# Third layer's opening: layer-norm statistics in two tiles, twelve token tiles normalised ahead of the last output products, first chunk in the blocks' order

## The chip, the core and the metric

The kernel runs on one core of one Trainium2 chip. A core has five engines that run their own queues in order: PE (matrix products; its weight loads are listed apart as PEld), DVE (vector work), ACT (activation functions and scaled copies), POOL and SP (here both mostly issue transfers). All data that the engines work on lie in an on-chip memory of 128 partitions; PE writes to a second, small one (PSUM), from which DVE and ACT read. The metric is the device time of one execution in microseconds, as the median of several runs.

## What is computed

Four layers on one sequence of L = 2048 tokens with D = 640 channels, each with a residual: a long convolution (a state-space model, evaluated with Fourier transforms), attention with 32 query heads of 20 channels that share one key and one value head, the same convolution again, the same attention again.

```python
    x = A_u
    x = x + _A_ref(_layernorm(x, axis=-1), A_A_re, A_A_im, A_B_re, A_B_im, A_C_re, A_C_im, A_log_dt, A_Dskip)
    x = x + _B_ref(_layernorm(x, axis=-1), B_wq, B_wk, B_wv, B_wo)
    x = x + _A_ref(_layernorm(x, axis=-1), A_A_re, A_A_im, A_B_re, A_B_im, A_C_re, A_C_im, A_log_dt, A_Dskip)
    x = x + _B_ref(_layernorm(x, axis=-1), B_wq, B_wk, B_wv, B_wo)
    return x
```

The layer norm has no weights: (x − mean) / sqrt(var + eps), with mean and variance over a token's 640 channels.

## The kernel before

**Where things lie.** x stays on the chip for the whole program, as 16 token tiles `x[:, t]` of 128 tokens by 640 channels. Each layer opens pools of tiles and gives them back at its end. Within a pool the places follow the order in which the code first asks for each tag, and a tile that is asked for waits only for the former tiles that lay in its own place. The layers' pools start at the same address. In the second layer (attention, `nm` = "b") there lie, in bytes per partition from that address: keys, values and queries up to 27,712; then the output weights `wo` (12,800) and `wol` (2,560); six probability tiles `pt` (24,576 together); two `on` tiles (4,096); two `rc` tiles (4,096); ten `ot` tiles (20,480). In the third layer (convolution, "c") the order before is B 16,384; R 8,192; xn 12,288; A1 16,384; kh 16,384; wi 32,768; A2 and A0 16,384 each. So xn lies on queries and `wo`, kh on `pt` and the first `on`, and wi on the second `on`, `rc` and `ot`.

**The end of an attention layer** (`main_loop`, L1128). The queries go in four blocks `nb` of four token tiles each; block `nb` owns the tiles `TAUS[4*nb : 4*nb+4]`, and with `FIRST = (0, 2, 1, 3)` these are the tiles t with t % 4 equal to `FIRST[nb]`. Per step PE computes scores (L1173), ACT exponentials (L1177) and PE the weighted values (L1187). Output products of the block before run one at a time between the steps, and `add` (L1230) adds each into x on DVE (L1235) and, when a tile is complete, calls `stats` (L625), which writes mean and variance of the tile into `mv` (L630, L631). Thus all tiles with t % 4 of 0, 2 and 1 are complete early in the last block, and only the four with t % 4 == 3 are left for the end. There, after the last exponential, `normalize_last` (L1219) divides the last heads on DVE (`rcl`, `onl`); PE meanwhile runs the other 28 output products (weights `wo`), then 16 with `onl` (weights `wol`), both at L1247 into the tiles `pl`; and eight additions with their statistics follow as the pairs of products end. The tiles `pl` 0 to 2 share the tag "s2" of three PSUM buffers with the tiles z of the convolution.

**The opening of a convolution layer** (`conv_layer`, L737). `norm` (L694) works on all 16 tiles at once: it adds eps (L705), takes the root on ACT (L687), a reciprocal with one correction step on DVE (L688 to L692), the offset (L707), and the negated scale and offset (L750, L751). Then for each chunk c of 128 channels `prepare` (L820) normalises the 16 token tiles into `xn` on ACT (L761; one buffer), `raw` (L563) runs four groups t of 32 products by the Fourier weights `wf` on PE (L574) into a PSUM tile z, and ACT copies each z into the spectrum A (L576). Group t reads the tiles t, t + 4, t + 8 and t + 12, so the group t = 3 reads the four last tiles. Chunks 0 and 1 use `raw`, later ones `dense`. `whole` gives DVE the work behind it: `halve` (L580) in four pieces for chunk 0, piece i after copy i, then the transform `fft8` (L114, L117), then the multiplication by the kernel's spectrum (L845 and on), whose tile kh is loaded on SP's queue at L711. The inverse transform's weights `wi` follow in the same queue (L555).

**What sets the order.** In `conv_layer` PE, ACT and DVE run in the order of the code. In `main_loop` PE and ACT do; DVE's order is worked out by a planner, which takes instructions in the code's order as they become ready in its own model of time. SP's queue is in order.

Of the kernel before, what the change touches and what calls it, by code (L numbers as in the profile page):

```python
# [11 lines left out]
F32 = mybir.dt.float32  # L12
# [3 lines left out]
AF = mybir.ActivationFunctionType  # L16
# [141 lines left out]
class Net:  # L158
# [7 lines left out]
    def setup(self, ctx):  # L166
# [8 lines left out]
        self.mv = self.xp.tile([P, 16, 2], F32, name="mv")  # L175
# [382 lines left out]
    def spectrum(self, nm, k):  # L558
        tag = f"A{k}" if k < 3 else "kh"
        return self.cvp.tile([P, 16, 256], F32, tag=tag, bufs=1, name=f"A{nm}")  # L560

    def raw(self, xn, nm, k):
# [4 lines left out]
        for t in range(4):  # L567
# [12 lines left out]
    def halve(self, A, pieces=1):  # L580
# [3 lines left out]
        for i in range(pieces):  # L584
# [5 lines left out]
    def whole(self, A, sg, pieces=1):  # L590

        return self.halve(A, pieces) + fft8(self.nc, A, self.B, sg, low=self.B[:, 8:16])
# [32 lines left out]
    def stats(self, t):  # L625
# [5 lines left out]
        nc.vector.bn_aggr(self.mv[:, t], st.rearrange("p a b -> p (a b)"))  # L631
# [62 lines left out]
    def norm(self, nm):  # L694
        rs = self.xp.tile([P, 16], F32, tag="rs", bufs=2, name=f"rs{nm}")
        nmr = self.xp.tile([P, 16], F32, tag="nmr", bufs=2, name=f"nmr{nm}")
        self.rstd(self.xp, self.mv, rs, nmr, 16)
        return rs, nmr

    def rstd(self, pool, mv, out, nmr, n):  # L700

        nc = self.nc
        ve = pool.tile([P, n], F32, tag="ve", bufs=2, name="ve")
        sq = pool.tile([P, n], F32, tag="sq", bufs=2, name="sq")
        nc.vector.tensor_scalar(ve, mv[:, :, 1], EPS, None, ALU.add)  # L705
        self.root(ve, sq, out)
        nc.vector.scalar_tensor_tensor(nmr, mv[:, :, 0], -1.0, out, op0=ALU.mult, op1=ALU.mult)  # L707
# [30 lines left out]
    def conv_layer(self, nm, first):  # L738
# [6 lines left out]
        with tc.manual_schedule(engines={mybir.EngineType.PE, mybir.EngineType.Activation,  # L745
                                         mybir.EngineType.DVE}):
            rs, nmr = self.norm(nm)
            rsm = self.xp.tile([P, 16], F32, tag="rsm", bufs=1, name=f"rsm{nm}")
            nmrm = self.xp.tile([P, 16], F32, tag="nmrm", bufs=1, name=f"nmrm{nm}")
            nc.vector.tensor_scalar(rsm, rs, -1.0, None, ALU.mult)  # L750
            nc.vector.tensor_scalar(nmrm, nmr, -1.0, None, ALU.mult)  # L751
            self.norm_next(nm)
            if first:
                self.kernel_spectra()
            R = self.scratch(nm)
# [4 lines left out]
            def normal(out, c, tau, r, b):  # L760
                nc.scalar.activation(out, X(c, tau), AF.Identity, scale=r[:, tau : tau + 1],  # L761
# [617 lines left out]
```

## Time and profile before

| | |
|---|---|
| median of 3 runs | 3023.3 us |
| lowest and highest | 3022.26 and 3024.99 us |
| profiled execution, its own time | 3024.13 us |
| its span in the profile | 3022.3 us |
| PE busy | 2769.4 us (92%) |
| ACT busy | 2421.5 us (80%) |
| DVE busy | 1384.6 us (46%) |
| mean granted PE clock | 0.951 |
| third layer, from the last product of the second to the fourth layer's first transposition | 1695.3 to about 1936.5 us |

All numbers but the first two rows are from one profiled execution. Times within it count from the start of its span. In its timeline a row gives the start, the duration, the engine, the line of the code, the operation with what it writes and reads, the count, and in brackets how long the engine had been idle before and what ended that wait. The granted clock is the share of PE's full clock that the chip allowed in a stretch. Matrix products are pipelined, so a busy PE is not PE at its peak.

### The profile page before, as it was taken

The numbers are of one execution on the slowest core, as the hardware profiler recorded it, in microseconds if no ns is written. First come the engines' busy times: TensorE is split into PE (matmuls) and PEld (weight loads), VectorE is DVE, ScalarE is ACT, GpSimd is POOL, SyncE is SP. The second block draws the span as 40 slices with busy tenths as digits, with TensorE's granted clock in tenths as the row PEclk, the third lists the DMA queues.
The fourth block names the chain that finished last, engine by engine and source line by source line (L and its number), as shares of the span: only waits on it lengthen the run. The fifth ranks groups of instructions, "written<-read, shape, count | busy, mean of one in ns | idle before, by whom it ended". The sixth has DMA issues, their size and how long they took to land. (4 is left out here: it accounts for less than half of the span.)

```text
span 3022.3 us, 52462 instructions
## 1 busy us (share of the span) xinstructions
PE 2769.4 (92%) x21696; PEld 1266.8 (42%) x21696; DVE 1384.6 (46%) x1784; ACT 2421.5 (80%) x2894; POOL 86.3 (3%) x149
## 2 busy tenths in 40 slices
PE   2676978898999999999999888798999999999999
PEld 0333978775233323333233678673233233333233
DVE  7999899942122232322323499721222223222223
ACT  5888351444999999999999524238999999999997
POOL 0001001000000000000000011000000000000000
PEclk9656999999999999999999989899999999999999
DMA  6114555433200010100000256131100100110100
GB/s 145 33 22 112 175 154 112 97 116 115 81 22 25 22 27 21 27 24 23 25 22 20 86 112 145 39 130 56 28 24 23 43 22 25 39 28 21 43 19 23
DMA packets 126000, 175.60 MB, mean 58 GB/s; under 512 B 59460, under 2 KB 81988, under 8 KB 122132
## 3 DMA queue, kind: packets, MB, share of 16 engines
q1 hardware_dynamic: 102680, 137.70, 15.7%
q0 software_dynamic: 21104, 33.45, 5.5%
q8 instruction: 175, 2.87, 0.4%
q10 hardware_dynamic: 1968, 0.98, 0.1%
q14 instruction: 73, 0.60, 0.1%
HBM read 95.22 MB, written 48.04 MB: 47 GB/s over the span
## 5 line engine op out<-in xcount | busy, mean ns | idle before, releaser
L1177 ACT ACTIVATE pt<-scd 128x1024 f32<-128x1024 f32 x1024 | 942.2, 1116 | 6.9 <-PE scd L1173 5.5
L1177 ACT ACTIVATE pt<-scb 128x1024 f32<-128x1024 f32 x1024 | 942.1, 1116 | 6.5 <-PE scb L1173 5.1
L1187 PE MATMUL pod<-pt,vt 128*32 128x512 f32 x4096 | 546.9, 606 | 4.4 <-DVE on L1204 0.2
L1187 PE MATMUL pob<-pt,vt 128*32 128x512 f32 x4096 | 546.4, 605 | 4.4
L1173 PE MATMUL scb<-qpb,kt 62*128 62x512 f32 x2048 | 385.8, 451 | 5.9 <-DVEq L1122 5.6
L1173 PE MATMUL scd<-qpd,kt 62*128 62x512 f32 x2048 | 385.7, 451 | 5.9 <-PEq L1122 5.5
L1173 PEld LDWEIGHTS scd<-qpd,kt 62*128 62x128 f32 x2048 | 166.1, 185 | 402.2 <-ACT pt L1177 392.4
L1173 PEld LDWEIGHTS scb<-qpb,kt 62*128 62x128 f32 x2048 | 166.1, 185 | 401.6 <-ACT pt L1177 391.9
L1235 DVE TENSOR_TENSOR x<-pyd,x 128x320 f32<-128x320 f32 x146 | 71.8, 492 | 560.7 <-PE pyd L1247 560.7
L1235 DVE TENSOR_TENSOR x<-pyb,x 128x320 f32<-128x320 f32 x146 | 71.8, 492 | 547.5 <-PE pyb L1247 547.5
L1207 DVE RECIPROCAL rc<-rc 128x512 f32<-128x512 f32 x62 | 207.9, 3353 | 2.1
L1187 PEld LDWEIGHTS pod<-pt,vt 128*32 128x32 f32 x4096 | 80.6, 108 | 177.4 <-issue 159.5
L1187 PEld LDWEIGHTS pob<-pt,vt 128*32 128x32 f32 x4096 | 80.6, 108 | 177.5 <-issue 159.5
L804 PE MATMUL yc<-Ac,wi 128*128 128x128 f32 x640 | 80.2, 291 | 32.1 <-DVE Ac L114 20.4
L804 PE MATMUL ya<-Aa,wi 128*128 128x128 f32 x640 | 79.8, 290 | 32.2 <-DVE Aa L114 22.8
L1247 PE MATMUL pyb<-wo,ot 128*32 128x320 f32 x1168 | 105.3, 432 | 0.0
L1247 PE MATMUL pyd<-wo,ot 128*32 128x320 f32 x1168 | 105.3, 432 | 0.0
L804 PEld LDWEIGHTS yc<-Ac,wi 128*128 128x128 f32 x640 | 79.7, 207 | 34.9 <-DVE x L815 11.8
L804 PEld LDWEIGHTS ya<-Aa,wi 128*128 128x128 f32 x640 | 79.1, 206 | 35.1 <-DVE Aa L114 24.0
L610 ACT ACTIVATE Aa<-za 128x1024 f32<-128x1024 f32 x12 | 12.3, 1025 | 101.6 <-PE za L608 101.6
L608 PE MATMUL zc<-xnc,wf 128*128 128x256 f32 x384 | 85.3, 384 | 2.4 <-ACT xnc L761 2.3
L608 PE MATMUL za<-xna,wf 128*128 128x256 f32 x384 | 83.7, 380 | 2.7 <-ACT xna L761 2.7
(323 smaller groups left out, 3110.3 us busy)
## 6 DMA issues: line engine op xcount, KB each, us to landing
Akh<-kh SPq DMA_DIRECT2D x10, 2048.0 KB
kh<-Ak SPq DMA_DIRECT2D x5, 2048.0 KB
qhd<-qh SPq DMA_DIRECT2D x40, 256.0 KB
qld<-ql SPq DMA_DIRECT2D x40, 256.0 KB
qpb<-qhd SPq DMA_DIRECT2D x256, 40.0 KB
qpd<-qhd SPq DMA_DIRECT2D x256, 40.0 KB
ot<-on SPq DMA_DIRECT2D x216, 40.0 KB
wf<-in_c_wf POOLq DMA_DIRECT2D x16, 512.0 KB, 8.0
```

What stands on the lines that cost most here:

```text
L608: nc.tensor.matmul(zv[:, :, c, kk], self.wf[:, t + 4 * h, j, c, kk], x, start=(n == 0), stop=(n == 3))
L610: nc.scalar.activation(A.rearrange("p (o s) d -> p o s d", o=2)[:, :, 2 * t : 2 * t + 2], z.rearrange("p (c o e) -> p o c e", c=2, o=2), A ...
L804: nc.tensor.matmul(y[:, s * DC : (s + 1) * DC], self.wi[:, t, j, c_, kk], v[:, 2 * t + c_, kk], start=(i == 0 and not whole), stop=(i == 3 ...
L1173: nc.tensor.matmul(sc[:, 512 * par : 512 * par + 512], kt[rows, 128 * t : 128 * t + 128], qps[nb, hg, pr][rows], start=True, stop=True)
L1177: nc.scalar.activation(pt, sc, AF.Exp, scale=SCALE)
L1187: nc.tensor.matmul(po[32 * j : 32 * j + 32], vt[:, t], pts[step, j // 2][:, 512 * (j % 2) : 512 * (j % 2) + 512], start=(t == 0), stop=(t ...
L1207: nc.vector.reciprocal(rc, rc)
L1235: nc.vector.tensor_tensor(xh, py, xh, ALU.add)
L1247: nc.tensor.matmul(py[j : j + m], o[:, 128 * i + j : 128 * i + j + m], w[:, 320 * half : 320 * half + 320], start=start, stop=stop)
```

## The change

`mv` becomes two tiles: `mv[0]` for the twelve token tiles with t % 4 in (0, 1, 2) and `mv[1]` for the four with t % 4 == 3; `place` maps a token tile to its tile and column. `norm(nm, g)` works on one of the two sets and also makes the negated scale and offset. In the first layer both sets are done where the one was. For the third layer `norm("c", 0)` stands at the end of the second layer's `main_loop`, after `normalize_last` and ahead of the last output products. In the third layer the tiles A1, A2 and xn are asked for ahead of R, kh and wi, so that the order of places becomes B, A1, A2, xn, R, kh, wi, A0. Chunk 0 is prepared in the order FIRST: the tiles of the groups 0 and 2 are normalised first, those of group 1 ahead of the first group's z, and, after that z and its copy, `norm("c", 1)` and the four tiles of group 3; `halve` takes its four pieces in the same order. Later chunks and the other layers keep their order.

```diff
--- before.py
+++ after.py
@@ -172,7 +172,9 @@
         nc.vector.memset(self.halfpi, 0.5 * math.pi)
         self.xp = ctx.enter_context(tc.tile_pool(name="xp", bufs=1))
         self.x = self.xp.tile([P, 16, D], F32, name="x")
-        self.mv = self.xp.tile([P, 16, 2], F32, name="mv")
+        self.mv = [self.xp.tile([P, 12, 2], F32, name="mv0"), self.xp.tile([P, 4, 2], F32, name="mv1")]
+        self.rn = None
+        self.placed = {}
         self.kd = self.dr.tile([NCH, P, 16 * DC], F32, name="kd")
         self.kh = self.dr.tile([NCH, P, 32 * DC], F32, name="kh")
 
@@ -556,15 +558,18 @@
                           self.ins[name][:, t * 1024 : (t + 1) * 1024])
 
     def spectrum(self, nm, k):
+        if nm in self.placed:
+            return self.placed.pop(nm)
         tag = f"A{k}" if k < 3 else "kh"
         return self.cvp.tile([P, 16, 256], F32, tag=tag, bufs=1, name=f"A{nm}")
 
-    def raw(self, xn, nm, k):
+    def raw(self, xn, nm, k, order=range(4), ahead=lambda t: None):
 
 
         nc = self.nc
         A = self.spectrum(nm, k)
-        for t in range(4):
+        for t in order:
+            ahead(t)
             z = self.ps2(f"z{nm}_{t}")
             zv = z.rearrange("p (h c k d) -> p h c k d", h=2, c=2, k=2)
             for h in (1, 0):
@@ -577,19 +582,19 @@
                                  z.rearrange("p (o c d) -> p o c d", o=2, c=2), AF.Copy)
         return A
 
-    def halve(self, A, pieces=1):
+    def halve(self, A, pieces=1, order=None):
 
 
         calls, n = [], 8 // pieces
-        for i in range(pieces):
+        for i in range(pieces) if order is None else order:
             lo, hi = A[:, n * i : n * i + n], A[:, 8 + n * i : 8 + n * i + n]
             for op, o in ((ALU.add, self.B[:, 8 + n * i : 8 + n * i + n]), (ALU.subtract, hi)):
                 calls.append(lambda o=o, lo=lo, hi=hi, op=op: self.nc.vector.tensor_tensor(o, lo, hi, op))
         return calls
 
-    def whole(self, A, sg, pieces=1):
-
-        return self.halve(A, pieces) + fft8(self.nc, A, self.B, sg, low=self.B[:, 8:16])
+    def whole(self, A, sg, pieces=1, order=None):
+
+        return self.halve(A, pieces, order) + fft8(self.nc, A, self.B, sg, low=self.B[:, 8:16])
 
     def dense(self, xn, nm, k):
 
@@ -628,7 +633,12 @@
         st = self.xp.tile([P, 2, 6], F32, tag="st", bufs=2, name=f"st{t}")
         for h in range(2):
             nc.vector.bn_stats(st[:, h], self.x[:, t, 320 * h : 320 * h + 320])
-        nc.vector.bn_aggr(self.mv[:, t], st.rearrange("p a b -> p (a b)"))
+        g, i = self.place(t)
+        nc.vector.bn_aggr(self.mv[g][:, i], st.rearrange("p a b -> p (a b)"))
+
+    def place(self, t):
+
+        return (1, t // 4) if t % 4 == 3 else (0, 3 * (t // 4) + t % 4)
 
     def stats_setup(self, nm):
 
@@ -691,20 +701,22 @@
         nc.vector.tensor_scalar(sq, sq, -0.5, 1.5, ALU.mult, ALU.add)
         nc.vector.tensor_tensor(out, out, sq, ALU.mult)
 
-    def norm(self, nm):
-        rs = self.xp.tile([P, 16], F32, tag="rs", bufs=2, name=f"rs{nm}")
-        nmr = self.xp.tile([P, 16], F32, tag="nmr", bufs=2, name=f"nmr{nm}")
-        self.rstd(self.xp, self.mv, rs, nmr, 16)
-        return rs, nmr
-
-    def rstd(self, pool, mv, out, nmr, n):
-
-        nc = self.nc
-        ve = pool.tile([P, n], F32, tag="ve", bufs=2, name="ve")
-        sq = pool.tile([P, n], F32, tag="sq", bufs=2, name="sq")
+    def norm(self, nm, g):
+
+        nc, n = self.nc, (12, 4)[g]
+        if g == 0:
+            self.rn = {}
+        rs, nmr, rsm, nmrm = (self.xp.tile([P, n], F32, tag=f"{k}{g}", bufs=1, name=f"{k}{g}{nm}")
+                              for k in ("rs", "nmr", "rsm", "nmrm"))
+        ve = self.xp.tile([P, n], F32, tag=f"ve{g}", bufs=1, name=f"ve{g}{nm}")
+        sq = self.xp.tile([P, n], F32, tag=f"sq{g}", bufs=1, name=f"sq{g}{nm}")
+        mv = self.mv[g]
         nc.vector.tensor_scalar(ve, mv[:, :, 1], EPS, None, ALU.add)
-        self.root(ve, sq, out)
-        nc.vector.scalar_tensor_tensor(nmr, mv[:, :, 0], -1.0, out, op0=ALU.mult, op1=ALU.mult)
+        self.root(ve, sq, rs)
+        nc.vector.scalar_tensor_tensor(nmr, mv[:, :, 0], -1.0, rs, op0=ALU.mult, op1=ALU.mult)
+        nc.vector.tensor_scalar(rsm, rs, -1.0, None, ALU.mult)
+        nc.vector.tensor_scalar(nmrm, nmr, -1.0, None, ALU.mult)
+        self.rn[g] = rs, nmr, rsm, nmrm
 
     def load_spectrum(self, c):
         A = self.spectrum(f"kh{c}", 3)
@@ -744,32 +756,37 @@
         tt = nc.vector.tensor_tensor
         with tc.manual_schedule(engines={mybir.EngineType.PE, mybir.EngineType.Activation,
                                          mybir.EngineType.DVE}):
-            rs, nmr = self.norm(nm)
-            rsm = self.xp.tile([P, 16], F32, tag="rsm", bufs=1, name=f"rsm{nm}")
-            nmrm = self.xp.tile([P, 16], F32, tag="nmrm", bufs=1, name=f"nmrm{nm}")
-            nc.vector.tensor_scalar(rsm, rs, -1.0, None, ALU.mult)
-            nc.vector.tensor_scalar(nmrm, nmr, -1.0, None, ALU.mult)
+            if first:
+                self.norm(nm, 0)
+                self.norm(nm, 1)
             self.norm_next(nm)
             if first:
                 self.kernel_spectra()
+            else:
+                for c in range(2):
+                    self.placed[f"{nm}{c}"] = self.spectrum(f"{nm}{c}", c + 1)
+                self.placed["xn"] = self.cvp.tile([P, 24, DC], F32, tag="xn", bufs=1, name=f"xn{nm}0")
             R = self.scratch(nm)
 
             def X(c, tau):
                 return self.x[:, tau, c * DC : (c + 1) * DC]
 
-            def normal(out, c, tau, r, b):
-                nc.scalar.activation(out, X(c, tau), AF.Identity, scale=r[:, tau : tau + 1],
-                                     bias=b[:, tau : tau + 1])
+            def normal(out, c, tau, neg=0):
+                g, i = self.place(tau)
+                r, b = self.rn[g][2 * neg : 2 * neg + 2]
+                nc.scalar.activation(out, X(c, tau), AF.Identity, scale=r[:, i : i + 1], bias=b[:, i : i + 1])
 
             def normals(xn, c, t):
 
                 for j in range(2):
                     i = 4 * j + t
-                    normal(xn[:, i], c, 8 * j + t, rs, nmr)
-                    normal(xn[:, 8 + 2 * i], c, 8 * j + t + 4, rs, nmr)
-                    normal(xn[:, 9 + 2 * i], c, 8 * j + t + 4, rsm, nmrm)
+                    normal(xn[:, i], c, 8 * j + t)
+                    normal(xn[:, 8 + 2 * i], c, 8 * j + t + 4)
+                    normal(xn[:, 9 + 2 * i], c, 8 * j + t + 4, 1)
 
             def new_xn(c):
+                if "xn" in self.placed:
+                    return self.placed.pop("xn")
                 return cv.tile([P, 24, DC], F32, tag="xn", bufs=1, name=f"xn{nm}{c}")
 
             def m(a, c_):
@@ -820,10 +837,26 @@
             def prepare(c):
 
                 xn = new_xn(c)
+
+                def group(t):
+                    for tau in (t + 4, t + 12, t, t + 8):
+                        normal(xn[:, tau], c, tau)
+
+                if c == 0 and not first:
+                    for t in FIRST[:2]:
+                        group(t)
+
+                    def ahead(t):
+                        if t == FIRST[0]:
+                            group(FIRST[2])
+                        elif t == FIRST[1]:
+                            self.norm(nm, 1)
+                            group(FIRST[3])
+
+                    return self.raw(xn, f"{nm}{c}", 1, FIRST, ahead)
                 for t in range(4):
                     if c < 2:
-                        for tau in (t + 4, t + 12, t, t + 8):
-                            normal(xn[:, tau], c, tau, rs, nmr)
+                        group(t)
                     else:
                         normals(xn, c, t)
                 return (self.raw if c < 2 else self.dense)(xn, f"{nm}{c}", (c + 1) % 3)
@@ -833,7 +866,7 @@
             self.wi = cv.tile([P, 8, 2, 2, 2, P], F32, tag="wi", name="wi")
             self.load_weights(self.wi, "c_wi", nc.sync)
             As[1] = prepare(1)
-            weave(self.whole(As[0], -1, 4), ())
+            weave(self.whole(As[0], -1, 4, None if first else FIRST), ())
 
             def spread(A, kh):
 
@@ -1275,6 +1308,8 @@
                 if (nb, hg, t) == (0, 1, 0):
                     late_loads(pts[steps[s + 2], 0])
             on = normalize_last()
+            if out is None:
+                self.norm("c", 0)
 
             last = []
             for g in range(3):
```

## The prediction

> **What bounds the kernel now.** I read the page first, then the chain of waits in order of time, then the timeline of the place where the second layer (attention) hands over to the third (convolution), then the windows of that place.
>
> ```profile
> span 3022.3 us, 52462 instructions
> ...
> PE 25%; issue 6%; DVE 1%; SPq 0%; DMA 0%; ACT 0%; POOL 0%; POOLq 0%; ACTq 0%
> ```
> ```profile
> 2057.69 1.95 ACT pt L1177 x2
> ```
>
> The first is the chain's share by engine, the second its earliest entry. The shares add to about a third of the span, which fits a chain that begins at 2057.69: it says nothing of the handover, which has to be read from the timeline (start, duration, engine, line, count, idle time before).
>
> ```profile
> 1682.15 1.28 ACT L687 ACT_TABLE_LOAD   x1
> ...
> 1683.18 7.80 PE L1247 MATMUL plb<-wo,ot 128*128 128x320 f32 x28
> ...
> 1683.32 0.73 DVE L1224 STREAM_SHUFFLE rcl<-pob 128x512 f32<-128x512 f32 x1
> 1683.35 0.36 SPq L711 DMA_DIRECT2D Akh<-kh  x1
> ...
> 1687.48 0.69 DVE L1227 TENSOR_TENSOR onl<-pob,rcl 128x512 f32<-128x512 f32 x1
> ...
> 1690.82 4.47 PE L1247 MATMUL plb<-wol,onl 128*128 128x320 f32 x16
> 1692.10 0.89 DVE L1235 TENSOR_TENSOR x<-plb,x 128x320 f32<-128x320 f32 x2 [3.93 <-PE plb L1247]
> ...
> 1695.32 3.98 SPq L555 DMA_DIRECT2D wi<-in_c_wi  x8
> ...
> 1697.51 0.44 DVE L1235 TENSOR_TENSOR x<-plb,x 128x320 f32<-128x320 f32 x1
> ...
> 1698.77 0.21 DVE L631 BATCH_NORM_AGGREGATE mv<-st 128x2 f32<-128x12 f32 x1
> 1699.01 0.17 DVE L705 TENSOR_SCALAR ve<-mv 128x16 f32<-128x16 f32 x1
> 1699.22 0.21 ACT L687 ACTIVATE sq<-ve 128x16 f32<-128x16 f32 x1 [15.79 <-DVE ve L705]
> ...
> 1700.80 0.17 DVE L751 TENSOR_SCALAR nmrmc<-nmrc 128x16 f32<-128x16 f32 x1
> 1700.85 6.26 ACT L761 ACTIVATE xnc<-x,nmrc,rsc 128x128 f32<-128x128 f32 x16 [1.42 <-DVE rsmc L750]
> ...
> 1701.40 16.87 PE L574 MATMUL zc<-xnc,wf 128*128 128x128 f32 x128 [6.11 <-ACT xnc L761]
> 1707.63 1.02 ACT L576 ACTIVATE Ac<-zc 128x1024 f32<-128x1024 f32 x1 [0.52 <-ACT xnc L761]
> ...
> 1711.16 1.02 ACT L576 ACTIVATE Ac<-zc 128x1024 f32<-128x1024 f32 x1 [2.50 <-PE zc L574]
> ...
> 1718.30 1.02 ACT L576 ACTIVATE Ac<-zc 128x1024 f32<-128x1024 f32 x1 [2.55 <-PE zc L574]
> 1719.22 6.26 ACT L761 ACTIVATE xnc<-x,nmrc,rsc 128x128 f32<-128x128 f32 x16
> ...
> 1719.76 14.72 PE L574 MATMUL zc<-xnc,wf 128*128 128x128 f32 x128 [1.49 <-ACT xnc L761]
> ...
> 1731.88 1.23 DVE L845 SCALAR_TENSOR_TENSOR Rc<-Ac,Akh 128x1024 f32<-128x1024 f32 x1
> ```
>
> The last output products end at 1690.82 + 4.47 = 1695.29. PE then waits 6.11 us for a strictly serial chain: last additions into x (to 1697.95), last statistics (to 1698.98), root and scales of all 16 token tiles, first normalised tiles. Nothing else runs under it: ACT had been idle for 15.79 us. From 1701.40 PE sets the pace: the four z groups of chunk 0 are copied out at 1707.63, 1711.16 and so on to 1718.30.
>
> Three of those steps take 3.55 us each (1718.30 − 1707.63 = 10.67), but the first group, from 1701.40 to 1707.6, took 6.2 us. The windows (stretch, its length, busy time and count of PE, weight load, DVE, ACT and POOL, granted clock, DMA share, GB/s) say why.
>
> ```profile
> 1699.00:1700.00 1.00, 0.00 (x0) 0.00 (x0) 0.64 (x4) 0.21 (x1) 0.00 (x0) 0.72 1.03 422
> ...
> 1706.00:1707.00 1.00, 1.00 (x10) 1.00 (x9) 0.00 (x0) 1.00 (x3) 0.00 (x0) 0.86 1.00 385
> ```
> ```profile
> 1774.00:1779.00 5.00, 0.00 (x0) 0.00 (x0) 4.90 (x6) 2.88 (x8) 1.66 (x2) 0.90 0.00 0
> ...
> 1791.00:1792.00 1.00, 1.00 (x8) 1.00 (x8) 0.00 (x0) 0.00 (x0) 0.00 (x0) 0.70 0.84 123
> ```
>
> The granted clock is either 1.00 or 0.50, so a mean gives the moment of the step: 0.72 puts the fall at 1699.44, 0.86 the rise at 1706.28. The wait therefore costs twice: 6.11 us of idleness, then 6.2 − 3.55 = 2.65 us of a halved clock.
>
> **The change part by part.** *Twelve tiles' scales move ahead of the last products.* Their tokens belong to the first three blocks, done long before. Nine DVE instructions and one ACT root now sit between the last softmax division and the additions. The root stands behind the last exponential and the table load, which it needed anyway: 1682.15 + 1.28 + 0.21 = 1683.64. The DVE part takes 1.54 us after the root (before: root end 1699.43, last scale end 1700.97). If the planner puts all of it ahead of the shuffle at 1683.32, onl moves by 1.86 us, from 1688.17 to 1690.03; if it all stands behind onl, it ends at 1690.2. PE wants onl at 1690.82, and DVE stands idle 3.93 us before 1692.10. Cost 0 either way; without this cover 1.9 us.
>
> *Twelve normalised tiles* take 6.26/16 = 0.39 us each. They begin at 1690.2 at the latest; four are ready at 1691.8, twelve at 1694.9, before PE is free at 1695.29. They need the new place of xn, last held by probability tiles, which PE has done with when it turns to the output products at 1683.18. That these writes wait for nothing else is worked out from the order of places, and without it the gain would shrink by what they are late beyond 1695.29.
>
> *PSUM for z.* The first three z groups take the banks of the last output tiles. The first pair of additions ends at 1692.99, the last of all at 1697.95, and the second z group begins only at 1698.84. No wait.
>
> *The last four tiles.* Aggregation ends at 1698.98, so ve is there at 1699.2. The root queues on ACT behind the first z copy: z ends at 1695.29 + 3.55 = 1698.84, copy to 1699.9, root to 1700.1. Before, root end to first tile took 1.42 us: 1701.5. Four tiles: 1703.1. Queued behind them is the second z copy (due 1702.4, now 1703.1), for which only DVE's halving waits. PE needs the four at 1695.29 + 3 × 3.55 = 1705.94. Spare 2.8 us; cost 0. A stray 3 us on DVE here would cost 0.2 us.
>
> *Order of halving* has the same eight DVE instructions; z order and halving order agree, so the last pair still starts right behind the last copy. Cost 0.
>
> *First layer.* Here the sixteen are still done together but as two sets: nine more DVE instructions, one more ACT root.
>
> ```profile
> 304.06 0.21 ACT L687 ACTIVATE sq<-ve 128x16 f32<-128x16 f32 x1 [2.79 <-DVE ve L705]
> ...
> 304.31 1.02 ACT L576 ACTIVATE Ak<-zk 128x1024 f32<-128x1024 f32 x1
> ...
> 305.65 0.17 DVE L751 TENSOR_SCALAR nmrma<-nmra 128x16 f32<-128x16 f32 x1
> 307.82 1.02 ACT L576 ACTIVATE Ak<-zk 128x1024 f32<-128x1024 f32 x1 [2.49 <-PE zk L574]
> ...
> 317.86 0.69 DVE L587 TENSOR_TENSOR B<-Ak 128x512 f32<-128x512 f32 x1 [12.04 <-DMA kd<-kst]
> ```
>
> DVE idles 12.04 us behind it, which hides the 2 us. The second root delays the copy of 304.31 to about 306.3; the next is due at 307.82. Cost 0; without these two covers 2 us.
>
> *Transfers.* The new order of places puts kh where wi began. The trace shows what that place waits for: wi was issued at 1695.32, the end of the last product that reads onl, while kh went at 1683.35. Now kh goes at 1695.3 and wi right behind it in SP's queue: 2 + 4 MB at once.
>
> ```profile
> 1686.00:1688.00 2.00, 2.00 (x9) 1.45 (x8) 1.97 (x2) 0.00 (x0) 0.00 (x0) 1.00 1.00 426
> ```
> ```profile
> 1695.40:1701.40 6.00, 0.00 (x1) 0.00 (x1) 5.05 (x21) 0.76 (x3) 0.00 (x0) 0.84 0.85 299
> 1701.40:1707.60 6.20, 6.20 (x34) 6.20 (x35) 0.00 (x0) 5.71 (x15) 0.00 (x0) 0.61 0.97 385
> ...
> 1736.00:1770.00 34.00, 33.11 (x161) 28.83 (x162) 33.65 (x37) 15.22 (x34) 5.18 (x4) 0.95 0.61 125
> 1770.00:1800.00 30.00, 18.34 (x119) 17.63 (x118) 27.94 (x34) 6.88 (x18) 5.10 (x4) 0.77 0.69 139
> ```
>
> kh is 2 MB and wi eight pieces of 512 KB, 6.3 MB together. At 299 to 426 GB/s, what these stretches show for the same loads, they take 15 to 21 us: all landed by 1717 even if kh came last. Its first reader, the multiplication of 1731.88, moves to 1723.2. Cost 0.
>
> *Sum.* PE starts chunk 0 at 1695.29 instead of 1701.40 (−6.11) and never falls to half clock (−2.65): the fourth copy comes at about 1709.6 instead of 1718.30, **−8.7 us**. Behind it DVE and PE are tied by data alone as far as the next layer, so the shift should stay: of 1736 to 1770 DVE is busy 33.65 us of 34. What is late next is the unchanged 1.49 us before chunk 1, whose tiles wait for the one xn buffer, and then DVE's transforms.
>
> *The clock term's bounds.* The four steps above (1699.44, 1706.28, 1778.0 from 0.90, 1791.6 from 0.70) lie 6.84, 71.7 and 13.6 us apart: 2, 21 and 4 times 3.42. The clock is judged on a grid of 3.42 us. Starting at 1695.29, an idle stretch of 6.11 us holds a whole grid interval in 8 placements of 10 ((6.11 − 3.42)/3.42), and then the halved clock lasts between one and two intervals of work, 3.4 to 6.8 us. Here it lasted 1706.28 − 1701.40 = 4.88 us and cost 2.65, or 0.54 per us. So the term lies between 0 and 3.7; I take the measured 2.65, since it goes with the execution from which the sum is made. The same grid moves the cold stretches further on (1785 to 1792, for instance) by about 1 us either way. The Trainium skill ("TensorE: Matmul & The Clock Gate", Part 1) says that windows of some 3.4 us run freely, are not started by the kernel, halve the clock after an idle one and restore it after a busy one. The trace agrees with the spacing; by that rule the term differs from run to run, and it speaks against counting all of 2.65; the first rival is what it would make of the time.
>
> **How the sum stands to the runs.** The profiled execution took 3024.13 us, 0.8 above the median of 3023.3. Its sum is 3024.13 − 8.7 = 3015.4; from the median it is 3014.6. I forecast the middle, **3015.0**.
>
> **Rivals.** (1) *The clock term is not there to be won*: the runs timed before fell mostly where the grid spares them. For it: 2 placements in 10, and a spread of 2.7 us between three runs. Against: the profiled run has it. Gain 6.1, time 3023.3 − 6.1 = 3017.2.
>
> (2) *The change doesn't get its head start*: ACT's reads of x count as waiting for all additions that stand ahead of them. Then tiles begin at 1697.95, PE at about 1698.5; idle 3.2 us is too short for a fall of the clock; gain 2.9 + 2.65 = 5.55, time 3017.7. Against it, in this trace:
>
> ```profile
> 1879.42 1.02 PE L797 MATMUL yc<-x,ident 128*128 128x512 f32 x2
> ...
> 1879.62 0.69 DVE L815 TENSOR_TENSOR x<-yc,x 128x512 f32<-128x512 f32 x1 [0.35 <-PE yc L804]
> ```
>
> PE reads x 0.2 us before an addition that precedes it in the program but touches other columns. Reads of x wait for their own region.
>
> (3) *Slower: kh becomes the wait.* Its load now stands behind the last product and shares the DMA engines with wi. It eats into the gain where kh lands after 1723.2 and makes the kernel slower where it lands past 1731.9: 36.6 us for 6.3 MB, below 172 GB/s. At the 139 GB/s of the stretch 1770 to 1800, which has other traffic, it would land at 1740.6, 8.7 us later than it is used now: time 3023.3 + 8.7 = 3032. Against: both loads moved at 299 GB/s or more in this place.
>
> **Chances.** Forecast 0.78; (1) 0.13; (2) 0.05; (3) and whatever else makes it slower 0.04. A measurement of this kernel tells about 0.2%, 6.0 us, from no change: faster means below 3017.3. All of the forecast and half of (1) lie there: 0.84. The other half of (1) and (2) are no change: 0.12. Slower: 0.04. The range runs from the lowest run with the largest gain and 1 us of later clock (3022.26 − 6.1 − 3.7 − 1 = 3011.5) to the profiled time without clock term (3024.13 − 6.1 = 3018.0).
>
> **What would show it.** Right: the wait of 6.11 us before line 574's first group is gone, that group takes 3.6 us at clock 1.00, roots of 12 and 4 elements stand near 1683.6 and 1700, the four last tiles end before 1706, kh is issued at about 1695.3 and DVE's first multiplication by it has no wait. Wrong: any wait on DMA before that multiplication, onl later than 1690.8, a stall within chunk 0's four groups, or a gain that is in the third layer's opening but gone before the fourth layer's first exponential.

## The result

| | median, us | lowest to highest | runs |
|---|---|---|---|
| before | 3024.01 | 3022.26 to 3025.65 | 12 |
| after | 3016.37 | 3015.45 to 3018.9 | 12 |

The ratio is 0.9976 [0.9968, 0.9983]: 7.6 us (0.24%) faster, with 5.1 to 9.7 in the interval. Timed again beside later experiments, the changed kernel took 3017.48 us against 3025.93, ratio 0.9973 [0.9963, 0.9984]. The profiled execution took 3017.37 us, its span is 3015.5 us and the mean granted clock 0.949.

### The profile page after: what moved, and what is told of

Read it like the earlier page. It is cut to its first block, busy times and chain, and to the rows that moved or that the text cites. A ratio compares the mean times of both kernels' runs of the same rounds, so it can differ in the third digit from the quotient of the medians.

```text
span 3015.5 us, 52490 instructions
## 1 busy us (share of the span) xinstructions
PE 2768.7 (92%) x21696; PEld 1263.8 (42%) x21696; DVE 1386.2 (46%) x1802; ACT 2421.6 (80%) x2896; POOL 86.3 (3%) x149
```

## The profile after

The timeline of the handover, columns as before.

```profile
1685.08 1.28 ACT L697 ACT_TABLE_LOAD   x1
...
1686.11 7.80 PE L1280 MATMUL plb<-wo,ot 128*128 128x320 f32 x28
...
1686.37 0.21 ACT L697 ACTIVATE sq0c<-ve0c 128x12 f32<-128x12 f32 x1
1686.88 0.21 DVE L698 RECIPROCAL rs0c<-sq0c 128x12 f32<-128x12 f32 x1
1687.02 3.35 DVE L1258 RECIPROCAL rcl<-rcl 128x512 f32<-128x512 f32 x1
...
1690.41 0.69 DVE L1260 TENSOR_TENSOR onl<-pob,rcl 128x512 f32<-128x512 f32 x1
...
1691.91 4.73 ACT L777 ACTIVATE xnc<-x,nmr0c,rs0c 128x128 f32<-128x128 f32 x12 [5.33 <-DVE rsm0c L717]
...
1693.75 4.47 PE L1280 MATMUL plb<-wol,onl 128*128 128x320 f32 x16
1695.03 0.89 DVE L1268 TENSOR_TENSOR x<-plb,x 128x320 f32<-128x320 f32 x2 [3.03 <-PE plb L1280]
...
1698.06 14.45 PE L579 MATMUL zc<-xnc,wf 128*128 128x128 f32 x128
1698.25 0.36 SPq L723 DMA_DIRECT2D Akh<-kh  x1
1698.67 7.82 SPq L557 DMA_DIRECT2D wi<-in_c_wi  x8
...
1701.83 1.02 ACT L581 ACTIVATE Ac<-zc 128x1024 f32<-128x1024 f32 x1 [5.19 <-PE zc L579]
...
1702.75 0.20 ACT L697 ACTIVATE sq1c<-ve1c 128x4 f32<-128x4 f32 x1
...
1704.18 1.65 ACT L777 ACTIVATE xnc<-x,nmr1c,rs1c 128x128 f32<-128x128 f32 x4 [1.24 <-DVE nmr1c L716]
...
1708.97 1.02 ACT L581 ACTIVATE Ac<-zc 128x1024 f32<-128x1024 f32 x1 [2.24 <-PE zc L579]
1712.55 1.02 ACT L581 ACTIVATE Ac<-zc 128x1024 f32<-128x1024 f32 x1 [2.55 <-PE zc L579]
...
1714.00 14.72 PE L579 MATMUL zc<-xnc,wf 128*128 128x128 f32 x128 [1.49 <-ACT xnc L777]
...
1726.13 1.23 DVE L878 SCALAR_TENSOR_TENSOR Rc<-Ac,Akh 128x1024 f32<-128x1024 f32 x1
```

The last output products end at 1693.75 + 4.47 = 1698.22, and the row of chunk 0's products has no bracket: PE goes straight on, where it had waited 6.11 us. (It starts 0.16 us before the modelled end of the products, which is how pipelined products are shown.) To compare kernels whose clocks have drifted apart by then, I measure the **opening** from the end of the last output product to the start of the fourth z copy. Before: 1718.30 − 1695.29 = 23.01 us. After: 1712.55 − 1698.22 = 14.33 us, 8.68 less. DVE's first multiplication by kh comes 27.91 us after the products instead of 36.59, again 8.68 less.

The windows of the first two z groups (stretch, length, busy time and count of PE, weight load, DVE, ACT, POOL, granted clock, DMA share, GB/s) have the clock, and a later one has the end of the transfers.

```profile
1698.06:1701.60 3.54, 3.54 (x33) 3.54 (x32) 3.54 (x11) 0.00 (x0) 0.00 (x0) 1.00 0.72 204
1701.60:1705.20 3.60, 3.60 (x34) 3.60 (x33) 2.43 (x13) 2.13 (x5) 0.00 (x0) 1.00 0.94 399
...
1712.00:1716.00 4.00, 2.51 (x21) 2.23 (x20) 2.36 (x3) 3.45 (x8) 0.00 (x0) 1.00 0.84 335
1716.00:1720.00 4.00, 4.00 (x38) 4.00 (x38) 3.93 (x7) 4.00 (x11) 0.00 (x0) 1.00 0.00 0
```

The first two groups take some 3.6 us each at clock 1.00. Nothing moves after 1716, so kh and wi have landed 10 us ahead of the multiplication at 1726.13, which has no wait.

The first layer, ACT's timeline:

```profile
304.28 0.21 ACT L697 ACTIVATE sq0a<-ve0a 128x12 f32<-128x12 f32 x1 [2.41 <-DVE ve0a L714]
...
306.10 0.20 ACT L697 ACTIVATE sq1a<-ve1a 128x4 f32<-128x4 f32 x1 [1.60 <-DVE ve1a L714]
306.21 1.01 ACT L581 ACTIVATE Ak<-zk 128x1024 f32<-128x1024 f32 x1
308.52 1.02 ACT L581 ACTIVATE Ak<-zk 128x1024 f32<-128x1024 f32 x1 [1.31 <-PE zk L579]
```

The second root holds one copy back to 306.21; the next still waits for PE and comes in its turn.

## The experiments

The theory was that of the prediction: the gain is PE's wait plus the halved clock behind it, and everything else is hidden. The rivals: the slow first group comes from the transfers beside it; the new order of places, or of z groups, is what counts; a hidden term isn't hidden. Each is compared with the kernel before, timed beside it.

**Is there a clock term?** In the kernel before, products that nobody reads fill PE's wait: first twelve, then six. The chunk's own data comes no earlier.

```diff
+            if not first:
+                fill = self.ps2("fill")
+                for _ in range(12):
+                    nc.tensor.matmul(fill[:, 0:512], self.ident,
+                                     self.wf[:, 0].rearrange("p a b c k -> p (a b c k)")[:, 0:512],
+                                     start=True, stop=True)
             As = {0: prepare(0)}
```

> The kernel before, with twelve products of 512 columns into a PSUM tile that nobody reads, put on PE between the last output product and chunk 0's first group (about 5.3 us of PE work inside the wait of 6.11 us). Theory (the wait costs twice, 6.11 us idle and 2.65 us of halved clock): the granted clock stays at 1.00, the first group takes 3.6 us instead of 6.2, the last z copy starts 20.4 us after the end of the last output product instead of 23.0; time 1.5 to 2.7 us below before. Rival (the first group is slow because of the 385 GB/s of the weight load in the same stretch, or because its tiles arrive one by one): the group stays near 6.2 us, the copy at 23.0, no change of the time.

Measured: 3027.84 us against 3025.27, ratio 1.001 [1.0001, 1.0019]. The size of the filler was a miss. Timeline of this kernel:

```profile
1695.74 10.46 PE L834 MATMUL fill<-wf,ident 128*128 128x512 f32 x24
1706.04 14.46 PE L574 MATMUL zc<-xnc,wf 128*128 128x128 f32 x128
```

One product is shown as two records and took 10.46/12 = 0.87 us, so the filler outlasted the wait and chunk 0 began 10.1 us after the last output product, 4.0 later than before. Its opening is 24.63 us, only 1.62 longer: behind the start, four groups took 2.4 us less than before. This doesn't separate the clock from the transfers yet: the loads had moved on while the filler ran, and beside this first group they ran at 192 GB/s only. Six products fit:

```diff
-                for _ in range(12):
+                for _ in range(6):
```

> The kernel before with six unread products on PE in the wait instead of twelve (the run with twelve showed 0.87 us each, so that they lasted past the wait; six are 5.2 us). Theory (the halved clock follows from PE's idleness): clock 1.00 throughout, first group 3.6 us, last z copy 23.0 - 2.65 = 20.4 us after the last output product, time 1.5 to 2.7 us below before. Rival (the load of wi, which runs under this group, slows it): the first group stays above 5 us and the copy near 23.0.

Measured: 3022.89 us against 3024.38, ratio 0.9996 [0.9987, 1.0005], so the total alone can't show it. Timeline of this kernel and window of its first group:

```profile
1695.18 5.31 PE L834 MATMUL fill<-wf,ident 128*128 128x512 f32 x12
...
1701.45 14.72 PE L574 MATMUL zc<-xnc,wf 128*128 128x128 f32 x128 [0.96 <-ACT xnc L761]
...
1716.21 1.02 ACT L576 ACTIVATE Ac<-zc 128x1024 f32<-128x1024 f32 x1 [2.55 <-PE zc L574]
```
```profile
1701.45:1705.29 3.84, 3.83 (x32) 3.75 (x33) 0.00 (x0) 3.84 (x11) 0.00 (x0) 1.00 1.02 414
```

The same 32 products in the first profile of the kernel before:

```profile
1701.40:1707.38 5.98, 5.98 (x32) 5.98 (x33) 0.00 (x0) 5.71 (x15) 0.00 (x0) 0.59 1.00 396
```

Chunk 0 starts as late as before, 6.1 us after the last product, but its first group takes 3.84 us at clock 1.00 while the DMA engines move 414 GB/s; before, it took 5.98 us at a mean clock of 0.59 beside 396 GB/s. The transfers don't slow it; the clock did. The opening is 20.86 us, 2.15 shorter than before: the size of the clock term. (The first copy is late, behind the sixteen tiles on ACT, but the fourth waits for PE again.)

**Are the new places needed?** The changed kernel without the early placing of A1, A2 and xn, so that xn lies on the second layer's output weights again and kh on its probability tiles.

```diff
-            else:
-                for c in range(2):
-                    self.placed[f"{nm}{c}"] = self.spectrum(f"{nm}{c}", c + 1)
-                self.placed["xn"] = self.cvp.tile([P, 24, DC], F32, tag="xn", bufs=1, name=f"xn{nm}0")
```

> The changed kernel with the tiles A1, A2 and xn asked for where they were before, so that xn lies on the output weights again and kh on the probability tiles. Theory (only the early scales and tiles matter): the twelve tiles start about 2 us later, when the last product with wo ends, but four are still ready before PE is free; kh is issued some 12 us earlier and nobody notices; last z copy 14.3 us after the last output product, the same as in the changed kernel; time 3016.4, within 1 us. Rival (the new places are what makes the head start possible): the first group waits, and up to 6.1 us come back, time up to 3022.5.

Measured: 3017.18 us, ratio 0.9976 [0.9967, 0.9985]; the opening is 14.32 us. ACT's timeline:

```profile
1692.42 4.73 ACT L773 ACTIVATE xnc<-x,nmr0c,rs0c 128x128 f32<-128x128 f32 x12 [7.37 <-PE plb L1276]
```

The twelve tiles now wait for the last product that reads `wo` and still start 4.27 us before the products end at 1696.69. The new places cost nothing and bring nothing here.

**Is the blocks' order worth anything?** Groups of chunk 0 in the order 0, 1, 2, 3, and halved in that order; the four late tiles stay last, as they are in both orders.

```diff
-                    for t in FIRST[:2]:
+                    for t in range(2):
...
-                    return self.raw(xn, f"{nm}{c}", 1, FIRST, ahead)
+                    return self.raw(xn, f"{nm}{c}", 1, range(4), ahead)
...
-            weave(self.whole(As[0], -1, 4, None if first else FIRST), ())
+            weave(self.whole(As[0], -1, 4), ())
```

> The changed kernel with chunk 0 in the order 0, 1, 2, 3 in preparation, products and halving. Theory (what counts is that the four late tiles are used by the last group, which holds in both orders): no change, last z copy 14.3 us after the last output product, time 3016.4 within 1 us. Rival (the blocks' order has a part in the gain): a wait of up to one group, 3.6 us, appears within chunk 0, time up to 3020.

Measured: 3017.23 us, ratio 0.9974 [0.9964, 0.9985], opening 14.33 us. The order is worth nothing.

**What does the place of the scales in the program bring?** `norm("c", 0)` moves from the end of the second layer to the start of the third.

```diff
+            self.norm(nm, 0)
             if first:
-                self.norm(nm, 0)
                 self.norm(nm, 1)
...
-            if out is None:
-                self.norm("c", 0)
```

> The changed kernel with the twelve tiles' scales moved from the end of the attention loop back to the start of the third layer; the split statistics, the places and the order stay. Theory A (DVE takes them behind the last additions and statistics, as the code has them): the first tiles start about 5.5 us after the last output product as before, the wait of some 6 us on PE and the fall of the clock are back, time 3023 to 3025. Theory B (the planner pulls them ahead of the last additions, since they depend only on the twelve's own statistics tile): the head start stays, time 3016.4 within 1 us, and the split alone would have been enough.

Measured: 3020.39 us, ratio 0.9984 [0.9975, 0.9994], about 3 us slower than the two versions of the changed kernel timed beside it (3017.18 and 3017.23). The opening stays at 14.33 us, so the head start was not lost. ACT's timeline inside the second layer shows where the time went:

```profile
1532.78 1.96 ACT L1210 ACTIVATE pt<-scb 128x1024 f32<-128x1024 f32 x2
1534.76 1.28 ACT L697 ACT_TABLE_LOAD   x1
1536.05 0.21 ACT L697 ACTIVATE sq0c<-ve0c 128x12 f32<-128x12 f32 x1
1536.28 1.28 ACT L1210 ACT_TABLE_LOAD   x1
1537.57 4.69 ACT L1210 ACTIVATE pt<-scb 128x1024 f32<-128x1024 f32 x5
```

The root is ready to run as soon as the twelve tiles are complete, and it went into the middle of the exponentials with a table load on either side, 2.8 us of the engine that sets the pace there (ACT is busy for 29.93 of the 30 us from 1500). Neither of the two expectations held as written. What the place behind `normalize_last` brings is a root behind the last exponential.

**How much spare do the four late tiles have?** Their scales and tiles one group later, then two groups later (the last moment).

```diff
-                        elif t == FIRST[1]:
+                        elif t == FIRST[2]:
```

> The changed kernel with the four late tiles behind the second z copy instead of the first. Theory (spare of 2.9 us): the four end about 0.7 us after the last group could start, but that group needs the first of them only at its start and the others later; no wait on PE, last z copy 14.3 us after the last output product; the third copy about 0.5 us late. Rival (all four are needed at once): PE waits 0.7 us or more.

Measured: one run, 3016.96 us; opening 14.33 us and no wait on PE. One whole group of spare is there.

```diff
-                        elif t == FIRST[1]:
+                        elif t == FIRST[3]:
```

> The changed kernel with the four late tiles' scales and tiles behind the third z copy of chunk 0, just ahead of the last group. Theory (PE alone bounds the opening, and the four tiles have 2.9 us to spare where the change has them): now they end the wait; first of them about 2.4 us after the third copy ends, PE stands still for about 3 us before the last group, last z copy 17.3 us after the last output product instead of 14.3; time 3 us above the changed kernel, 3019.5. Rival (PE is not the bound, DVE's halves and transform behind it have slack too): part of the 3 us is hidden, time below 3018.

Measured: 3021.23 us, ratio 0.9989 [0.998, 0.9998]; opening 19.32 us, 5.0 more than the changed kernel and 2 more than I expected. Timeline and windows:

```profile
1709.95 5.63 PE L579 MATMUL zc<-xnc,wf 128*128 128x128 f32 x32 [2.94 <-ACT xnc L777]
```
```profile
1707.44:1710.86 3.42, 0.91 (x6) 0.83 (x7) 2.42 (x10) 2.18 (x6) 0.00 (x0) 1.00 1.04 420
...
1710.00:1711.00 1.00, 1.00 (x7) 0.91 (x8) 0.97 (x3) 1.00 (x3) 0.00 (x0) 0.93 1.02 406
...
1714.00:1715.00 1.00, 1.00 (x10) 1.00 (x9) 0.00 (x0) 0.00 (x0) 0.00 (x0) 0.86 0.00 0
```

The wait is the 2.94 us that I expected, but the last group took 5.63 us instead of 3.6. The mean of 0.93 puts a fall of the clock at 1710.86, the 0.86 a rise at 1714.28, 3.42 us later. PE had been busy for 0.91 us of the 3.42 that ended with the fall, 27%. So an interval need not be wholly idle for the clock to fall. This overturns a step of the prediction, below.

**Is the clock term there every time?** The kernel before, unchanged, a second time.

> The kernel before, profiled once more. Theory (the clock is judged on a grid that runs on its own): the wait of 6.1 us is there again, but the halved stretch is another one, between 0 and 6.8 us of work, and the last z copy comes between 20.4 and 24.1 us after the last output product; the first two layers and the stage behind the opening take another 0 to 3 us more or less. Rival (the fall is tied to the program): 4.9 us of halved clock and 23.0 us again, to 0.1 us.

Measured: one run, 3025.21 us: wait 6.11 us, opening 1719.25 − 1696.30 = 22.95 us, the fall at 1700.34. It came 4.04 us after the last product, 4.15 in the first profile and 4.37 in the run with 192 bytes more below. The last product itself came 1.0 us later than in the first profile. So the rival's numbers came, and not a spread from 20.4 to 24.1. The clock records say why. With the grid continued from the recorded steps, a step lies 0.55 to 1.18 us behind the last product in all 13 profiles of this study, though against the start of the span the steps lie anywhere from 0.03 to 3.03 us. The wait of 6.11 us therefore holds a whole grid interval each time, and no run shows what another placement would do.

**Why is the changed kernel late before it reaches its gain?** Its last output product ends at 1698.22, 2.93 us later than before, though nothing ahead of it was to change but the first layer's scales. DVE's product `wr`, one of its first operations (7.59 us before, 8.33 after), is already late, by 0.74 us, and it waits for a load. `mv` as two tiles with the new scale tiles makes the resident pool 64 bytes shorter per partition, so every tile behind it moves by 64 bytes; the addresses in the built programs put the targets of the first loads on a multiple of 256 bytes before and on one of 64 after. Tested both ways: the changed kernel with 64 bytes more, and the kernel before with 192 bytes more (the added columns hold nothing).

```diff
-        self.mv = [self.xp.tile([P, 12, 2], F32, name="mv0"), self.xp.tile([P, 4, 2], F32, name="mv1")]
+        self.mv = [self.xp.tile([P, 12, 2], F32, name="mv0"), self.xp.tile([P, 12, 2], F32, name="mv1")]
...
-        mv = self.mv[g]
+        mv = self.mv[g][:, 0:n]
```

> The changed kernel with one difference: the statistics tile of the four late token tiles is 96 bytes per partition instead of 32 (only its first four columns are used). With that the resident pool is as long as in the kernel before, and every tile behind it, the targets of the first loads too, lies at the kernel before's address, a multiple of 256 bytes; in the changed kernel the same tiles lie 64 bytes lower. The opening of the third layer is expected unchanged: last z copy 14.3 us after the end of the last output product. Theory (the changed kernel's first loads, 290 GB/s between 5 and 6 us where the kernel before has 346, are slow because of where they are written): 346 GB/s again, DVE's work at 54.8 us of the kernel before back within 0.2 us of it (the changed kernel's profiles have it 0.2 to 0.6 later), and the time about 0.5 us below the changed kernel's, near 3016. Rival (the first loads' rate goes with something else in the changed program, or differs by chance): 290 GB/s as before, no shift at 54.8 us, same time as the changed kernel.

> The changed kernel itself, a second time, beside the version with 64 bytes more. Both theories of the first loads: last z copy 14.3 us after the last output product; loads between 5 and 6 us at 290 GB/s; time about 3016.4 to 3017.2. If the loads differ by chance, this profile or the next may show 346.

```diff
-        self.mv = self.xp.tile([P, 16, 2], F32, name="mv")
+        self.mv = self.xp.tile([P, 40, 2], F32, name="mv")
...
-        self.rstd(self.xp, self.mv, rs, nmr, 16)
+        self.rstd(self.xp, self.mv[:, 0:16], rs, nmr, 16)
```

> The kernel before with a statistics tile that is 192 bytes per partition longer (the added columns are not used), so that all tiles behind it lie 64 bytes below a multiple of 256, as in the changed kernel. Theory (the places of the first loads set their rate): 290 GB/s between 5 and 6 us instead of 346, DVE's work at 54.8 us some 0.5 us later, time 0.5 us above the kernel before, a ratio of about 1.0002. Rival (another cause in the changed program): 346 GB/s, no shift. In both, the third layer's opening is that of the kernel before: wait 6.11 us, last z copy 23 us after the last output product.

A window of the start, the last column in GB/s, and DVE's wait for the load, in this order: before; after; after with 64 bytes more; before with 192 more.

```profile
5.00:6.00 1.00, 0.00 (x0) 0.00 (x0) 0.33 (x2) 0.00 (x0) 0.00 (x0) 1.00 1.15 346
```
```profile
7.59 0.83 DVE L239 TENSOR_TENSOR wr<-rA_C_re,rA_B_re 128x640 f32<-128x640 f32 x1 [0.85 <-DMA rA_B_re<-in_A_B_re]
```
```profile
5.00:6.00 1.00, 0.00 (x0) 0.00 (x0) 0.06 (x1) 0.00 (x0) 0.00 (x0) 1.00 1.22 290
```
```profile
8.33 0.83 DVE L241 TENSOR_TENSOR wr<-rA_C_re,rA_B_re 128x640 f32<-128x640 f32 x1 [1.32 <-DMA rA_B_re<-in_A_B_re]
```
```profile
5.00:6.00 1.00, 0.00 (x0) 0.00 (x0) 0.19 (x1) 0.00 (x0) 0.00 (x0) 1.00 1.15 345
```
```profile
7.72 0.82 DVE L241 TENSOR_TENSOR wr<-rA_C_re,rA_B_re 128x640 f32<-128x640 f32 x1 [0.84 <-DMA rA_B_re<-in_A_B_re]
```
```profile
5.00:6.00 1.00, 0.00 (x0) 0.00 (x0) 0.00 (x0) 0.00 (x0) 0.00 (x0) 1.00 1.22 289
```
```profile
8.37 0.82 DVE L239 TENSOR_TENSOR wr<-rA_C_re,rA_B_re 128x640 f32<-128x640 f32 x1 [1.28 <-DMA rA_B_re<-in_A_B_re]
```

The rate goes with the place, in both programs. Over all profiles of this study, the five kernels with the old places have this operation at 7.49 to 7.99 us, the eight with the shifted ones at 8.04 to 8.52. DVE's work around 54.8 us keeps about half a microsecond of it (means 54.7 and 55.2), though the ranges overlap a little there: 54.57 to 55.00 against 54.93 to 55.53.

| | median, us | ratio to before [interval] | opening, us |
|---|---|---|---|
| before, timed beside these | 3025.93 | | |
| after with 64 bytes more | 3015.38 | 0.9966 [0.9954, 0.9978] | 14.33 |
| after, again | 3017.48 | 0.9973 [0.9963, 0.9984] | 14.33 |
| before with 192 bytes more | 3025.57 | 1.0 [0.9991, 1.0009] | 23.12 |

The version with 64 bytes more has the lowest median of all, but its interval overlaps that of the changed kernel, and its counterpart, the kernel before with shifted places, is no slower than the kernel before. The half microsecond is shown in the profiles, and not in the totals.

## Why the prediction was right

**The sum.** 8.7 us was predicted for the fourth copy, 8.68 measured; less the 2.93 us of drift, that copy stands at 1712.55 − 2.93 = 1709.62, predicted 1709.6. The wait of 6.11 us is gone, which leaves 8.68 − 6.11 = 2.57 us for the term taken as 2.65. Not all of it is the clock. The run with six unread products has the same wait at full clock and gains 2.15 us: that is the clock's part. Of the other 0.42 us, 0.27 is a slow start of products behind a wait (14.72 us for four groups in that run and in chunk 1, 14.45 without a wait), whose cause no run tests, and the rest is that the row after starts 0.16 us ahead of the modelled end of the products. The prediction put the whole difference, 6.2 − 3.55, down to the clock; its own figure of 0.54 per us is more than a clock of one half can cost. The size came out because the change removes all three parts.

**The hidden terms.** Counted from the last product, the twelve tiles begin 6.31 us ahead (5.1 predicted as the latest) and end 1.58 ahead. onl stands 4.99 us after the start of the `wo` products, as before, so the scales didn't delay it: one reciprocal slipped ahead of the long one and one product ahead of onl, the rest went behind it. The root stands 0.3 us after the start of those products, behind the table load. The z groups run on without a wait for PSUM. The first late tile comes 5.96 us after the last product (6.2 predicted) and the fourth is done at 7.61, when the last z group needs it at about 10.65: 3.0 us of spare, 2.8 predicted, borne out by the run one group later. kh went 0.03 us after the last product, wi behind it, and about 17 us later both had landed (15 to 21 predicted). The first layer's second root delayed one copy to 306.21 (306.3 predicted) and no other. The wait of 1.49 us before chunk 1 comes next, as named.

**Where the gain stays.** The fourth layer's first exponential comes 2057.69 − 1718.30 = 339.39 us after the fourth copy before; in the profile after:

```profile
2050.79 4.69 ACT L1210 ACTIVATE pt<-scd 128x1024 f32<-128x1024 f32 x5 [4.39 <-PE scd L1206]
```

That is 338.24 us after it. Nothing is given back on the way.

**What the total holds.** In the two profiles, of before and after, the span fell by 6.8 us: −8.68 in the opening, +2.93 ahead of it, and −1.05 behind it. Of the 2.93, 0.6 is there at 54.8 us, behind the first loads. All of it is there when the clock rises for the last time ahead of the handover, at 743.72 us before and 747.01 after, 3.29 apart, by these windows (before, then after):

```profile
743.00:744.00 1.00, 1.00 (x8) 0.19 (x8) 0.00 (x0) 0.73 (x1) 0.00 (x0) 0.64 0.44 141
```
```profile
746.00:748.00 2.00, 2.00 (x14) 0.50 (x12) 0.00 (x0) 1.81 (x2) 0.00 (x0) 0.75 0.17 47
```

From this rise to the last product the two take 951.57 and 951.21 us, and all profiles 951.2 to 951.8, but for the run with the root among the exponentials: 954.55, which is its 3 us. Over the profiles with the shifted places (the run with the root among the exponentials left out) the last product ends anywhere from 1696.06 to 1698.22, mean 1696.96, over those with the old places from 1695.29 to 1696.30, mean 1695.76. The means differ by 1.2; the rest of the 2.93 is scatter between executions. It arises ahead of the clock's last rise, which in the same twelve profiles lies anywhere from 743.62 to 747.01 us, 3.4 us apart. That fits a clock that rises only at steps of the grid; no run moved the grid to test it. The 8.68 us of the opening lie within the interval of 5.1 to 9.7 us for the whole kernel, so the medians don't contradict it; they don't measure it either.

**Wrong: how the clock term is bounded.** The prediction let the clock fall only where the idle stretch "holds a whole grid interval in 8 placements of 10", took 0 as the term's lower end, and gave the first rival 0.13. In the run with the tiles at the last moment an idle stretch of 2.94 us sufficed, in an interval that was 27% busy. However a stretch of 6.11 us lies on a grid of 3.42, one interval has at least 6.11/2 = 3.05 us of it, at most 11% busy. By that measure the fall comes every time, as it does by the bound in the last section; all three profiles of the kernel before's opening that I have show it (23.01, 22.95 and, with 192 bytes more, 23.12 us). Nor is the placement free: a step lies 0.55 to 1.18 us behind the last product in every profile. The forecast was closer to certain than I made it, and the first rival hardly existed. The same error stands in the second rival, where an idle stretch of 3.2 us was called "too short for a fall of the clock". With a loss like the one measured (2.94 us of wait and 2.05 of a slower last group) that rival would have gained some 3.7 us and not 5.55. It did not occur: the tiles begin 3.1 us ahead of the first addition.

**Not foreseen: the first loads.** The list of what the change touches left out that a pool made shorter moves everything behind it.

## What to carry to other kernels

A wait of PE costs more than its length when it is long enough for the clock to fall (a bound from these traces stands below): price the wait and the slow group behind it together, and test it by filling the wait with products that nobody reads. When work is pulled ahead, keep a root or any other function with its own table out of a loop of exponentials, by a place in the order written out by hand; here that was worth about 3 us of the 8. And when tiles of a resident pool change size, look at where the first loads now land: 64 bytes more per partition gave the rate back here, though the totals show no gain from it.

## What the hardware showed that I had not expected

**The clock falls after less than a whole idle interval.** The fall of 1710.86 followed a stretch of 3.42 us with PE busy for 0.91. The Trainium skill ("TensorE: Matmul & The Clock Gate", Part 1) has the clock return to half rate after at least one idle window of about 3.4 us; here an idle stretch of 2.94 us did it, and the measurement decides. The traces bound it further. I cut the time at full clock in all 13 profiles into the grid's intervals, some 10,000, of which 209 end with a fall. None with PE busy for less than 42% was spared, and none with PE busy for more than 58% was followed by a fall. (Busy time is modelled, so the two can overlap.) The two extremes, each with the interval behind it: the changed kernel falls after 1.97 of 3.41 us, and the kernel before, a second time, doesn't after 1.44 of 3.42.

```profile
262.32:265.73 3.41, 1.97 (x53) 0.94 (x52) 3.38 (x4) 3.38 (x4) 0.16 (x1) 1.00 0.00 0
265.73:269.15 3.42, 2.20 (x35) 0.95 (x34) 3.42 (x4) 3.39 (x5) 0.00 (x0) 0.50 0.02 5
```
```profile
437.40:440.82 3.42, 1.44 (x7) 0.93 (x5) 3.35 (x6) 1.94 (x4) 0.00 (x0) 1.00 1.01 431
440.82:444.23 3.41, 0.00 (x0) 0.00 (x0) 3.38 (x2) 3.41 (x10) 0.00 (x0) 1.00 0.16 67
```

**Loads slow down when their targets move by 64 bytes.** The first loads ran at 346 GB/s onto multiples of 256 bytes and at 290 GB/s 64 bytes lower, with the DMA engines fully busy in both cases (shares of 1.15 and 1.22). The Trainium skill ("DMA: Bandwidth & Descriptors", How a descriptor splits into AXI transactions) says that the first transaction of a transfer which doesn't start at a multiple of 256 bytes begins at the boundary below, and that the bytes ahead of the start are fetched for nothing. It says so of reads, while here the targets moved, so it agrees in direction only; it gives no rate.
